# Ordering a fused attention and MLP kernel's instructions with another simulated clock

## The chip, the cores and the metric

The kernel runs on one core of a Trainium2 chip. The metric is device time in microseconds, from launch to end of one execution; the time of a kernel is the median of several runs. Five engines work side by side, each from a queue of its own: TensorE (PE, with its weight loads as PEld), VectorE (DVE), ScalarE (ACT), GpSimd (POOL) and SyncE (SP, which here only issues DMAs).

## The reference

A recurrent attention over 768 time steps for 4 batches and 8 heads of size 40, and behind it a dense MLP from 320 to 2048 to 320 over the 3072 tokens. All in float32.

```python
def _attn_ref(r, k, v, w, a, b):
    state = zeros((B, H, D, D))
    for t in range(S):
        y[:, :, t] = einsum('bhd,bhde->bhe', rt, state)
        Sa = einsum('bhde,bhe->bhd', state, at)
        state = state * wt[:, :, None, :] - einsum('bhd,bhe->bhde', Sa, bt)
        state = state + einsum('bhd,bhe->bhde', vt, kt)
    return y

def _moe_ref(x, w_in, w_out):
    h = x @ w_in
    sp = where(h > 20.0, h, log1p(exp(minimum(h, 20.0))))
    return ((h * tanh(sp)) @ w_out)
```

## The kernel before

The 768 time steps are cut into 12 chunks of 64 (`C`). Within a chunk the recurrence is solved in closed form; only the state goes from one chunk to the next. The 32 pairs of batch and head are worked on together, in halves called `be` and `al`. The names of the parts, with their lines:

- `pre_a(c, be)` (126 to 203) prepares half a chunk. SP loads `wa` and `bk` (131, 134; two buffers each). VectorE forms products of the decays by scans (147, 157) and scales the inputs (152, 170), ScalarE copies `ad` (155), POOL stores `P` to DRAM as `pD` (172), TensorE makes the 64 by 64 products `pa` (186) and transposes (202), and ScalarE and VectorE take them out (188 to 193, 203).
- `pre_inv(n)` (205 to 221) inverts triangular blocks for a pair of chunks on VectorE: a transpose (209), 30 links of two dependent instructions each (214, 216), and transposes back (218, 220). It has one buffer each for `XL`, `tmp` and `TT`. Called the solve below.
- `post_inv(n)` (223 to 260) builds the block inverses with many small matmuls (232, 241) and copies (235, 249 to 251), and makes `KT` (258, 260).
- `step(c)` (349 to 370) carries the state over chunk `c`, for two halves `g`: `step_a` (copies of the state into `VS`, 277; matmuls `pu`, 284; `UVT`, 286), `step_u` and `step_d` (transposes, 293 and 304), `step_b` (matmuls `pq`, 314; masked copy `UVQ`, 316), and `step_c` (matmuls, 334 and 339; new state `ST`, 342 and 346; output `yev`, 343). `step_loads` (265 to 271) has POOL load `VS`, `UVT` and `bdr` for the next chunk, and POOL stores `yev` to DRAM as `yD` (370).
- `Mlp` (479 to 626). Its weights come as float32 and are split into a high and a low part by `split` (489 to 495), a chain of a DMA on SP (453), ScalarE (459, 494) and VectorE (461 to 463, 495) for each of 20 pieces. `run` then goes over 6 blocks of 512 tokens: SP loads `xy` and `xp` (472 to 476), VectorE and ScalarE make `xh` and `xl` (567 to 570), and for each of 8 parts of the hidden width come 16 matmuls `ph` (584), the activation (586), the split into `gh` and `gl` (589, 590), and, three parts later, 24 matmuls `po` (604 to 606). The results are copied and stored (610, 611).

What sets the order: the program is written as one long trace in the order of `attention`'s main loop (392 to 411), where each pair of chunks runs step, preparation of the pair after next (`a`), solve of the next pair (`i`), weight work (`A`), step. The MLP stands behind all of it. The framework then makes the order of each engine's queue itself. It keeps the data's dependences and the buffers, and picks among the instructions that are ready on a simulated clock by their priority, which is the place in the trace unless a block is moved ahead. That is done by hand all over the attention:

```python
def at(tc, k):
    return tc.high_priority(offset=OFF[k]) if OFF.get(k) else nullcontext()
...
    def inv(n):
        with at(tc, 'I%d' % n), at(tc, 'I'):
            TT, T1 = pre_inv(n)
        with at(tc, 'J%d' % n):
            post_inv(n, TT, T1)
```

`OFF` (38 to 40) holds some thirty such offsets, from -150 to 600: 600 for the first solve, 300 for the others, 80 more for each; 15 to 250 for parts of a step; 600 and 400 for the two blocks of weight work. The loads and stores of the attention go to the queues named by `QS = "SGGG"`: `wa` and `bk` on SP, everything else on POOL.

Of the kernel before, what the change touches and what calls it, by code (L numbers as in the profile page):

```python
# [47 lines left out]
def layouts(inp, S=768):  # L48
    nch = S // C

    def v(x):
        return x[:, :, :S].reshape(4, 2, 2, 2, nch, C, 40)

    r, k, vv, w, a, b = (v(inp[n]) for n in 'rkvwab')
    o = {}
    wt = w.transpose(4, 2, 1, 6, 3, 0, 5).reshape(nch, 2, 2, 40, 8, C)
    wa = np.zeros(wt.shape[:4] + (1040,), np.float32)
    wa[..., :520].reshape(wt.shape[:4] + (8, 65))[..., 1:] = wt
    wa[..., 528:] = a.transpose(4, 2, 1, 6, 3, 0, 5).reshape(nch, 2, 2, 40, 512)
    o['wa'] = wa  # L60
    bt, kt = (x.transpose(4, 2, 1, 6, 3, 0, 5).reshape(nch, 2, 2, 40, 8, 1, C) for x in (b, k))
    bk = np.concatenate([bt, kt], -2)
    bk[:, 1] = np.concatenate([kt, bt], -2)[:, 1]
    o['bk'] = bk.reshape(nch, 2, 2, 40, 8, 128)
    o['rD'] = np.ascontiguousarray(r.transpose(4, 1, 6, 2, 3, 0, 5)).reshape(nch, 2, 40, 16, C)
    o['vD'] = np.ascontiguousarray(vv.transpose(4, 1, 6, 3, 0, 2, 5)).reshape(nch, 2, 40, 8, 128)
    o['vN'] = np.ascontiguousarray(vv.transpose(4, 2, 5, 3, 0, 1, 6)).reshape(nch, 2, C, 16, 40)
    p = np.arange(128)
    cst = np.zeros((128, 328), np.float32)
    cst[:, :128] = np.eye(128)  # L70
    cst[:, 128:192] = (p[:, None] % 64) < np.arange(64)
    cst[:, 192:256] = np.arange(64) < (p[:, None] // 64) * 32 + p[:, None] % 32
    cst[:, 256:296] = (p[:, None] % 64) == np.arange(40)
    cst[:, 296:328] = np.arange(32) < p[:, None] % 32
    o['cst'] = cst
    return o
# [356 lines left out]
def mlp_layouts(inp):  # L433
    wi, wo = inp['moe_w_in'], inp['moe_w_out']
    wi = wi.reshape(2, 2, 2, 40, 2048).transpose(1, 3, 0, 2, 4).reshape(320, 2048)
    a = np.empty((128, 3, 2048), wi.dtype)
    a[:, 0], a[:, 1] = wi[0:128], wi[128:256]
    a[0:64, 2] = a[64:128, 2] = wi[256:320]
    o = {'wi': a.reshape(128, 3, 4, 512).transpose(0, 2, 1, 3), 'wo': wo.reshape(16, 128, 320).transpose(1, 0, 2)}
    o = {n: np.ascontiguousarray(x).reshape(128, -1) for n, x in o.items()}  # L440

    return {n: x.view(np.int64) if x.dtype == np.float64 else x for n, x in o.items()}
# [186 lines left out]
def build(tc, I, out, nch):  # L629
    with ExitStack() as ctx:  # L630
        dp = ctx.enter_context(tc.tile_pool(name="dp", bufs=1, space=bass.MemoryType.DRAM))
        yD = dp.tile([nch, 2, 40, 2, 512], F32, name="yD")
        pD = dp.tile([nch, 2, 40, 2, 520], F32, name="pD")
        M = Mlp(ctx, tc, I, yD, pD, out)
        with ExitStack() as actx:
            attention(actx, tc, I, yD, pD, nch, M)
        M.run(nch)


def launch(**inputs):  # L640
    import concourse.bacc as bacc
    import concourse.tile as tile
    from concourse.bass_utils import run_bass_kernel_spmd

    nch = inputs['r'].shape[2] // C
    arrays = layouts(inputs, nch * C)
    arrays.update(mlp_layouts(inputs))
    nc = bacc.Bacc("TRN2", target_bir_lowering=False, num_devices=1)
    I = {n: nc.dram_tensor("in_" + n, x.shape, mybir.dt.from_np(x.dtype), kind="ExternalInput").ap() for n, x in arrays.items()}
    out = nc.dram_tensor("out_0", (nch * 256, 320), F32, kind="ExternalOutput").ap()  # L650
    with tile.TileContext(nc) as tc:
        build(tc, I, out, nch)
    res = run_bass_kernel_spmd(nc, [{"in_" + n: x for n, x in arrays.items()}], core_ids=[0]).results[0]["out_0"]
    return np.ascontiguousarray(res.reshape(nch, 4, C, 320).transpose(1, 0, 2, 3)).reshape(nch * 256, 320)
# [4 lines left out]
```

## Time and profile before

| | us |
|---|---|
| median of 3 runs | 827.55 |
| lowest and highest run | 823.36 and 829.61 |
| span of the profiled execution, first to last instruction | 821.8 |
| first matmul | 14.97 |
| first and last solve begin (line 209) | 49.9 and 368.3 |
| first and last new state (line 346) | 128.5 and 459.4 |
| first matmul of the MLP | 460.65 |

The span is the only time that is recorded of the profiled execution itself; a run's time takes in a little on both sides of it. Times in rows are microseconds from the span's start. In a timeline row stand start, length, engine, line, operation and tiles; a bracket holds the idle time of the engine before it and whose end ended it. A wait row gives the total, the number and the longest of the waits of one line for another. In the 40 slices of the page each digit is the busy share in tenths, and PEclk the TensorE clock that was granted.

The chain that ended last is TensorE for 52% of the span, ScalarE for 9%, VectorE for 7% and DMA for 3%.

### The profile page before, as it was taken

The numbers are of one execution on the slowest core, as the hardware profiler recorded it, in microseconds if no ns is written. First come the engines' busy times: TensorE is split into PE (matmuls) and PEld (weight loads), VectorE is DVE, ScalarE is ACT, GpSimd is POOL, SyncE is SP. The second block draws the span as 40 slices with busy tenths as digits, with TensorE's granted clock in tenths as the row PEclk, the third lists the DMA queues.
The fourth block names the chain that finished last, engine by engine and source line by source line (L and its number), as shares of the span: only waits on it lengthen the run. The fifth ranks groups of instructions, "written<-read, shape, count | busy, mean of one in ns | idle before, by whom it ended". The sixth has DMA issues, their size and how long they took to land.

```text
span 821.8 us, 17217 instructions
## 1 busy us (share of the span) xinstructions
PE 722.7 (88%) x7048; PEld 644.8 (78%) x7048; DVE 458.7 (56%) x957; ACT 428.7 (52%) x931; POOL 103.4 (13%) x182
## 2 busy tenths in 40 slices
PE   2635798899889889888786899999999999999997
PEld 2524697788778778788676789999999999999997
DVE  6689878749899757988954558311312212111110
ACT  5533556784586867567685555343333333432331
POOL 8100012123223022221102100000000000000000
PEclk9855679999999999999999999999999999999999
DMA  6522224323433134423528755210300100000000
GB/s 169 143 65 81 57 53 96 99 67 97 118 103 76 59 96 105 83 58 111 142 76 207 160 157 135 59 51 1 77 33 0 55 17 1 33 1 1 33 1 32
DMA packets 58206, 61.81 MB, mean 75 GB/s; under 512 B 25536, under 2 KB 48704, under 8 KB 58128
## 3 DMA queue, kind: packets, MB, share of 16 engines
q1 hardware_dynamic: 49296, 40.94, 18.3%
q0 software_dynamic: 8832, 19.79, 10.0%
q8 instruction: 55, 0.90, 0.5%
q14 instruction: 23, 0.19, 0.1%
HBM read 48.79 MB, written 11.86 MB: 74 GB/s over the span
## 4 chain that ended last, share of the span: by engine, by line
PE 52%; ACT 9%; DVE 7%; DMA 3%; issue 2%; SPq 0%; ACTq 0%; DVEq 0%
PE ph L584 21%; PE po L605 7%; PE po L604 7%; PE po L606 7%; PE pa L258 2%; PE pa L186 2%; DMA xp<-pD 1%; DVE tmp L214 1%; DVE XL L216 1%; PE pq L314 1%; ACT bdT L249 1%; PE pu L284 1%; ACT bdT L250 1%; DMA cv_d<-in_wi 1%; ACT KT L260 1%
## 5 line engine op out<-in xcount | busy, mean ns | idle before, releaser
L590 DVE TENSOR_TENSOR gl<-g,gh 128x1024 fp32r<-128x1024 f32 x48 | 58.6, 1224 | 207.5 <-ACT gh L589 207.5
L586 ACT ACTIVATE g<-ph 128x512 f32<-128x512 f32 x96 | 57.3, 598 | 180.5 <-PE ph L584 180.3
L186 PE MATMUL pa<-bk,ad 128*128 128x168 f32 x384 | 85.6, 376 | 42.8 <-DVE bk L170 15.0
L604 PE MATMUL po<-w_oh,gh 128*128 128x320 f32 x384 | 118.3, 308 | 0.0
L605 PE MATMUL po<-w_ol,gh 128*128 128x320 f32 x384 | 118.3, 308 | 0.0
L606 PE MATMUL po<-w_oh,gl 128*128 128x320 f32 x384 | 118.3, 308 | 0.0
L584 PE MATMUL ph<-xh,w_ih 128*128 128x512 f32 x288 | 112.7, 393 | 2.0 <-ACT xh L568 2.0
L186 PEld LDWEIGHTS pa<-bk,ad 128*128 128x128 f32 x384 | 71.5, 235 | 48.2 <-issue 22.8
L584 PE MATMUL ph<-xh,w_il 128*128 128x512 f32 x288 | 97.1, 391 | 0.0
L584 PE MATMUL ph<-xl,w_ih 128*128 128x512 f32 x192 | 75.1, 391 | 0.0
L605 PEld LDWEIGHTS po<-w_ol,gh 128*128 128x128 f32 x384 | 72.1, 188 | 2.2
L604 PEld LDWEIGHTS po<-w_oh,gh 128*128 128x128 f32 x384 | 72.1, 188 | 1.8
L606 PEld LDWEIGHTS po<-w_oh,gl 128*128 128x128 f32 x384 | 72.1, 188 | 0.0
L584 PEld LDWEIGHTS ph<-xh,w_ih 128*128 128x128 f32 x288 | 54.1, 188 | 12.1 <-ACT xh L568 2.2
L584 PEld LDWEIGHTS ph<-xh,w_il 128*128 128x128 f32 x288 | 54.0, 188 | 11.6 <-issue 0.2
L216 DVE TENSOR_TENSOR XL<-XL,tmp 128x30 f32<-128x30 f32 (+9 forms) x180 | 58.7, 326 | 2.4
L214 DVE TENSOR_TENSOR tmp<-XL 128x30 f32<-128x30 f32 (+9 forms) x180 | 58.2, 324 | 2.3
L258 PE MATMUL pa<-bdT,HA 128*104 128x128 f32 x384 | 52.2, 289 | 7.0 <-ACT bdT L251 5.5
L258 PEld LDWEIGHTS pa<-bdT,HA 128*104 128x104 f32 x384 | 46.7, 179 | 11.1 <-ACT bdT L251 7.2
L314 PE MATMUL pq<-bdr,UVT 128*128 128x128 f32 x384 | 53.4, 284 | 0.4 <-ACT UVT L286 0.3
L334 PE MATMUL pq<-UVQ,bkn 128*64 128x104 f32 (+1 forms) x768 | 44.7, 254 | 7.8 <-DVE UVQ L316 5.5
L589 ACT CAST gh<-g 128x1024 fp32r<-128x1024 f32 x48 | 50.1, 1048 | 1.3
(89 smaller groups left out, 1212.6 us busy)
## 6 DMA issues: line engine op xcount, KB each, us to landing
wa<-in_wa SPq DMA_DIRECT2D x48, 162.5 KB
bk<-in_bk SPq DMA_DIRECT2D x48, 160.0 KB
cv_d<-in_wi SPq DMA_DIRECT2D x12, 512.0 KB
cv_d<-in_wo SPq DMA_DIRECT2D x8, 640.0 KB
pD<-P POOLq DMA_DIRECT2D x48, 81.2 KB, 2.2
VS<-in_vN POOLq DMA_DIRECT2D x24, 160.0 KB, 3.4
UVT<-in_vD POOLq DMA_DIRECT2D x24, 160.0 KB, 3.9
bdr<-in_rD POOLq DMA_DIRECT2D x24, 160.0 KB, 4.4
```

Source lines behind the costliest of these rows:

```text
L186: PE.matmul(pt[:, j], ad[:, s0 + j].rearrange("p k a t -> p (k a t)"), bk[:, s0 + j], start=(j == 0), stop=True, skip_group_check=True)
L214: V.tensor_tensor(out=tv, in0=X[:, i + 1:32, i:i + 1].broadcast_to([128, 31 - i, i]), in1=X[:, i:i + 1, 0:i].broadcast_to([128, 31 - i, i] ...
L216: V.tensor_tensor(out=X[:, i + 1:32, 0:i], in0=X[:, i + 1:32, 0:i], in1=tv, op=ALU.add)
L258: PE.matmul(pk[:, j], ha[:, s0 + j], bd[:, s0 + j].rearrange("p a t -> p (a t)"), start=(j == 0), stop=True, skip_group_check=True)
L314: PE.matmul(pq[:, s], UVT[:, g * 4 + s, be * 128:be * 128 + 128], br[:, be, g * 4 + s].rearrange("p a t -> p (a t)"), start=(s == 0), stop ...
L584: PE.matmul(ph, w, x, start=(n == 0), stop=(n == 7), skip_group_check=True)
L586: A.activation(g[:, j], ph, AF.Mish)
L589: A.copy(gh, g)
L590: V.tensor_tensor(out=gl, in0=g, in1=gh.bitcast(F32), op=ALU.subtract)
L604: PE.matmul(po[k], gh[:, j, t], oh, start=(f == 0), stop=False, skip_group_check=True)
L605: PE.matmul(po[k], gh[:, j, t], ol, start=False, stop=False, skip_group_check=True)
L606: PE.matmul(po[k], gl[:, j, t], oh, start=False, stop=(f == 15), skip_group_check=True)
```

## The change

The framework's context gets one argument. With it, the simulated clock that drives the ordering of the instructions is that of the framework's timeline simulator instead of the simulator that it takes by default. The trace, the priorities, the tiles and their buffers stay as they are.

```diff
-    with tile.TileContext(nc) as tc:
+    with tile.TileContext(nc, schedule_with_timeline_sim=True) as tc:
         build(tc, I, out, nch)
```

## The prediction

> **What bounds the kernel now.** The page comes first, for the span, the busy shares and the 40 slices.
>
> ```profile
> span 821.8 us, 17217 instructions
> PE 722.7 (88%) x7048; PEld 644.8 (78%) x7048; DVE 458.7 (56%) x957; ACT 428.7 (52%) x931; POOL 103.4 (13%) x182
> PE   2635798899889889888786899999999999999997
> PEclk9855679999999999999999999999999999999999
> ```
>
> TensorE is busy for 722.7 us of 821.8, so 99.1 us of the span are its idle time. The slices show that these are not spread evenly: from slice 23 on it stands at 9. The stages with their busy times come next, one row for each stretch; behind the stretch come its length and then the busy time of each engine.
>
> ```profile
> core 0: us, PE busy (x) PEld busy (x) DVE busy (x) ACT busy (x) POOL busy (x), PEclk, DMA share, GB/s
> 0.00:100.00 100.00, 51.18 (x251) 43.07 (x253) 80.88 (x183) 45.23 (x123) 24.61 (x46) 0.74 0.39 106
> 40.00:100.00 60.00, 32.51 (x163) 27.23 (x165) 52.99 (x130) 24.85 (x73) 5.07 (x10) 0.63 0.24 70
> 100.00:460.00 360.00, 315.29 (x4722) 278.95 (x4716) 280.02 (x682) 246.00 (x614) 75.19 (x131) 0.97 0.38 97
> 300.00:340.00 40.00, 37.17 (x465) 33.22 (x464) 31.36 (x82) 23.76 (x66) 13.72 (x24) 1.00 0.38 92
> 340.00:380.00 40.00, 33.85 (x503) 29.89 (x502) 33.40 (x88) 27.75 (x75) 5.81 (x12) 0.96 0.34 86
> 420.00:460.00 40.00, 30.02 (x490) 26.06 (x490) 21.01 (x37) 25.22 (x52) 7.14 (x11) 1.00 0.69 158
> 460.00:480.00 20.00, 19.35 (x197) 16.02 (x198) 11.05 (x13) 10.46 (x18) 2.86 (x5) 0.91 0.66 134
> 480.00:800.00 320.00, 320.00 (x1781) 290.59 (x1780) 85.57 (x79) 123.11 (x172) 0.75 (x2) 1.00 0.14 41
> 800.00:822.00 22.00, 16.91 (x109) 16.17 (x107) 1.23 (x1) 3.95 (x7) 0.00 (x0) 0.95 0.08 30
> ```
>
> So there are three stages. The start, 0 to 100, has 48.8 us of idle TensorE (100 - 51.18), and VectorE with 80.88 is the busiest engine there. The steady part of the attention, 100 to 460, has 44.7 us of idle TensorE (360 - 315.29). The MLP from 480 on has none until the tail, which has 5.1 (22 - 16.91). Then the waits between 100 and 460 (total, times, longest), for how the idle time is made up, and the longest of TensorE's in the timeline.
>
> ```profile
> POOL pD L172 <- DVE w L150: 66.8, 6, 18.2
> POOL VS L267 <- PE pu L284: 57.7, 12, 11.8
> PE pu L293 <- ACT UVT L286: 8.1, 7, 2.6
> PE pq L334 <- DVE UVQ L316: 5.5, 4, 3.1
> ```
> ```profile
> 452.46 0.94 PE L334 MATMUL pq<-UVQ,bkn 128*64 128x104 f32 x16 [3.15 <-DVE UVQ L316]
> ```
>
> The reader is to see that TensorE's waits are many and short, at most 3.15 us: hand-overs along chains of dependent work, not an engine stuck for long behind a badly placed instruction. Long waits stand only on POOL's queue, which has room.
>
> **The change, part by part.** No instruction, byte, buffer or priority is added or removed. What can move is the place of an instruction in its engine's queue, SP's and POOL's included, since both sorts of scheduler pick among the ready instructions by the written priorities, at the instants of a simulated clock. A different clock gives different instants, so other instructions are ready when an engine comes free. The program that reaches the chip holds each engine's instructions in the order so found. The price of the change is thus a change in TensorE's idle time, stage by stage.
>
> *MLP, 480 to the end: 0 us.* TensorE is busy for all 320.00 us up to 800. All its inputs but the next x block are made by ACT (123.11 of 320) and VectorE (85.57 of 320), so those cover any order of theirs; if that cover went, a late x block would show as a TensorE gap. The tail's 5.1 us are the last copy and store, in data order. Bounds: from 0 down, since there is nothing to win, to a few tenths up.
>
> *Start, 0 to 100: 0 us, between -25.7 and +10.6.* The first steps wait for the first triangular solve (the loop of lines 211 to 216 between the transposes of lines 209 and 218). Its groups on the page, for six solves together:
>
> ```profile
> L216 DVE TENSOR_TENSOR XL<-XL,tmp 128x30 f32<-128x30 f32 (+9 forms) x180 | 58.7, 326 | 2.4
> L214 DVE TENSOR_TENSOR tmp<-XL 128x30 f32<-128x30 f32 (+9 forms) x180 | 58.2, 324 | 2.3
> L209 DVE STREAM_TRANSPOSE XL<-GP 128x1024 f32<-128x1024 f32 x6 | 12.7, 2121 | 0.0
> L218 DVE STREAM_TRANSPOSE TT<-XL 128x1024 f32<-128x1024 f32 x6 | 11.7, 1950 | 0.1
> ```
>
> One solve is (58.7 + 58.2 + 12.7 + 11.7) / 6 = 23.6 us of VectorE. In the timeline of VectorE the first one lasts from 49.93 to 99.26:
>
> ```profile
> 49.93 2.09 DVE L209 STREAM_TRANSPOSE XL<-GP 128x1024 f32<-128x1024 f32 x1
> 51.90 1.20 DVE L147 TENSOR_TENSOR_SCAN P<-wa,d 128x520 f32<-128x520 f32 x1
> 53.05 0.17 DVE L214 TENSOR_TENSOR tmp<-XL 128x30 f32<-128x30 f32 x1
> ...
> 53.14 0.16 DVE L150 COPY w<-P 128x8 f32<-128x8 f32 x1
> 53.21 0.68 DVE L152 TENSOR_TENSOR wa<-wa,P 128x512 f32<-128x512 f32 x1
> 53.81 0.20 DVE L216 TENSOR_TENSOR XL<-XL,tmp 128x30 f32<-128x30 f32 x1
> ...
> 97.33 1.93 DVE L218 STREAM_TRANSPOSE TT<-XL 128x1024 f32<-128x1024 f32 x1
> ```
>
> That is 49.3 us, 25.7 more than its own work, because work of lines 147 to 170 for later chunks stands between its links. An order without that work would win up to 25.7 us here. An order with one more stall of the longest kind costs the 10.61 us of this TensorE row:
>
> ```profile
> 60.89 4.77 PE L186 MATMUL pa<-bk,ad 128*128 128x168 f32 x16 [10.61 <-ACT ad L155]
> ```
>
> I take 0, nearest to the row of VectorE: it is busy for 52.99 of 60 us, and what is moved out of the solve has to be done soon after, by the same engine.
>
> *Steady attention, 100 to 460: +12.6 us, between -20.6 and +60.1.* TensorE has 315.29 us of work here whatever the order, so the stage lasts that long divided by its busy share. The rows bound the share. The fullest stretch, 300 to 340, has 37.17 / 40 = 0.929; at that share the stage would last 339.4 us, 20.6 less. The emptiest, 420 to 460, where VectorE too is only busy for 21.01 of 40, has 0.751: 420.1 us, 60.1 more. The present mean is 0.876. I take 340 to 380, 33.85 / 40 = 0.846, the poorest stretch in which solves, preparation and steps still run side by side: 372.6 us, 12.6 more. The reason for a value on the dear side is an asymmetry in the rows. A better order can only take from waits that are short and partly true hand-overs. A worse one puts an instruction with an unmet wait at the head of a queue and holds up everything behind it; the POOL rows show what such a wait can be, 18.2 us. Behind a `pD` store on POOL's queue stand the loads of the next step (lines 267 to 271), and the first matmuls of that step (line 284) wait for those. On SP's queue the loads of `x` stand among the weight loads in the same way; that start of the MLP lies within this stage and its bounds.
>
> *Sum.* 0 + 0 + 12.6 on the span of 821.8 gives 834.4. The median, 827.55, lies 5.75 above that span (the runs lie 1.6 to 7.8 above it), so the forecast is 827.55 + 12.6 = 840.2, taken as 840.
>
> **The rivals.** *Faster, 809 us.* Place: the last solve. Its transposes:
>
> ```profile
> 368.27 2.13 DVE L209 STREAM_TRANSPOSE XL<-GP 128x1024 f32<-128x1024 f32 x1
> ...
> 408.52 1.98 DVE L218 STREAM_TRANSPOSE TT<-XL 128x1024 f32<-128x1024 f32 x1
> ```
>
> It lasts 42.2 us, 18.6 more than its own 23.6, and the last two steps and the half-empty stretch of 420 to 460 come after it. If the new clock calls the next link ready sooner, the solve runs unmixed, the weight conversions that were mixed in go into VectorE's free 19 us of 420 to 460, and the attention ends 18.6 us sooner: 827.55 - 18.6 = 809. For it: the other work is of low urgency. Against it: the written priorities already put the solve first, and it is mixed all the same. It decides once that solve takes under 30 us.
>
> *No change, 827.6 us.* The order may come out nearly as it is, because the data fix it: twelve steps in a row, six solves in a row, single buffers. For it: 315.29 us of TensorE work and 280.02 of VectorE's in 360 leave little freedom. Against it: with several chains running beside each other, few ties have to flip. This is also the case in which the change does not do what it says.
>
> *Much slower, 888 us.* One mechanism: on POOL's queue a `pD` store of a later chunk comes ahead of the next step's loads. At 5 us for each of 12 steps that is 60, the 60.1 of the bound above: 827.55 + 60.1 = 888. For it: POOL already waits 66.8 us in six such places. Against it: today the loads land in time, and TensorE has no long wait for them. It decides when the loads are issued later than the steps ahead of them end.
>
> *The clock falls, 865 us.* TensorE was granted 0.63 where it was busy for 32.51 of 60 us, and 1.00 where it was busy for 30.02 of 40. The row of line 186 above takes 4.77 / 16 = 0.298 us for each matmul at the low clock; at the full one it is 1.98 / 12 = 0.165:
>
> ```profile
> 337.09 1.98 PE L186 MATMUL pa<-bk,ad 128*128 128x168 f32 x12
> ```
>
> If on top of the forecast the emptiest stretch fell to the low clock, its 30.02 us of work would take 30.02 x (0.298 / 0.165 - 1) = 24.2 us more: 864.4, say 865. For it: a worse order brings gaps longer than the present 3.15 us. Against it: even 0.751 busy holds 1.00. The Trainium skill, in "TensorE: Matmul & The Clock Gate", section "What's actually happening", says that the array runs at half rate after an idle window of about 3.4 us and at the full rate again after a busy one. By that rule every gap of that length would cost clock as well as the gap, which speaks against any reordering; the trace agrees so far as waits of up to 3.15 us left the clock at 1.00 and the start with its 10.61 us wait had 0.63.
>
> **How the numbers follow.** Chances: the forecast (840) 0.35, no change 0.23, faster 0.22, much slower 0.15, the clock 0.05. About 1% is what a measurement of this kernel can tell from no change, so faster (below 819) is 0.22, the same 0.23, slower (above 836) 0.35 + 0.15 + 0.05 = 0.55. The range goes from the faster rival, 808, to the much slower one, 888; about half of each of these two cases lies outside it, some 0.2 in all. The likeliest case alone reaches from 828 to 855, from no loss to about twice the forecast one.
>
> **What would show it.** Right: TensorE's busy time within 1% of 722.7, no gap from 480 us after the start of the MLP on, and 100 to 460 longer by about 13 us with more waits of 1 to 4 us. The instruction counts must be the same. A last solve of under 30 us shows the faster rival, TensorE's waits for a DMA at line 284 the much slower one, a granted clock below 0.9 between 140 and 460 the clock's. I am wrong in the stage if the difference stands in the start or the MLP, and wrong in the sign if the steady stage's busy share rises above 0.876.

## The result, and the profile after

| | before | after |
|---|---|---|
| median, us | 825.99 (4 runs, 823.36 to 829.61) | 885.17 (4 runs, 882.48 to 889.0) |
| ratio | | 1.0717, 95% interval 1.0674 to 1.0761 |
| span of the profiled execution, us | 821.8 | 880.7 |
| first and last new state (line 346), us | 128.5 and 459.4 | 152.7 and 518.7 |
| first matmul of the MLP (line 584), us | 460.65 | 519.6 |

The kernel became 7.2% slower, 59 us. The three moments in the lower rows, which are starts in the timelines, divide the 59 us: the first new state comes 24.2 us later, the way from the first to the last one takes 366.0 us instead of 330.9, 35.1 us more, and the MLP takes 361.1 us from its first matmul to the end in both kernels. The page of the kernel after, its summary lines:

```profile
span 880.7 us, 17240 instructions
PE 739.5 (84%) x7048; PEld 664.4 (75%) x7048; DVE 462.5 (53%) x957; ACT 426.1 (48%) x931; POOL 103.3 (12%) x182
PE   1675339887877989886779869999999999999997
PEclk9667659999988988998798989999999999999999
```

The counts of busy instructions on every engine are those of before. TensorE's idle time is 880.7 - 739.5 = 141.2 us instead of 99.1, 42.1 more. The other 16.8 us of the longer span are TensorE's own work: the same 7048 matmuls took 739.5 us instead of 722.7, at a mean granted clock of 0.911 instead of 0.953. The stages of the kernel after (behind the stretch come its length and the busy time of each engine), and below them the fourth stretch in the kernel before:

```profile
0.00:100.00 100.00, 54.62 (x234) 46.20 (x235) 71.76 (x159) 46.13 (x124) 25.43 (x48) 0.76 0.39 111
40.00:100.00 60.00, 38.98 (x174) 32.95 (x173) 44.64 (x108) 27.87 (x83) 6.75 (x14) 0.70 0.29 87
100.00:460.00 360.00, 280.74 (x3986) 253.00 (x3985) 266.25 (x664) 210.02 (x540) 65.89 (x116) 0.87 0.29 77
140.00:460.00 320.00, 264.02 (x3715) 237.94 (x3714) 232.85 (x582) 198.03 (x513) 64.87 (x114) 0.91 0.32 84
560.00:880.00 320.00, 315.79 (x1778) 288.12 (x1776) 79.47 (x74) 117.62 (x167) 0.00 (x0) 1.00 0.11 32
```
```profile
140.00:460.00 320.00, 278.78 (x4191) 246.23 (x4189) 247.16 (x599) 219.82 (x552) 67.48 (x117) 0.99 0.39 100
```

Compare the third busy time, VectorE's, in the first two rows: 71.76 where it was 80.88, and 44.64 where it was 52.99. The engine that paces the start stands still for 9.1 us longer in the first 100 us and so gets fewer instructions done (159 instead of 183). TensorE is not worse off in these 100 us (54.62 against 51.18); what it loses comes right behind them, when it waits for VectorE's first solve. What VectorE stands still for is in the waits of the whole kernel (total, times, longest):

```profile
POOL VS L267 <- PE pu L284: 137.7, 14, 36.2
DVE w L145 <- DMA wa<-in_wa: 40.1, 19, 4.2
DVE cv_w L461 <- ACT cv_m L459: 30.9, 16, 7.0
PE pa L232 <- DVE TT L218: 22.1, 3, 20.2
DVE bk L170 <- DMA bk<-in_bk: 16.7, 10, 3.5
PE pq L314 <- DMA bdr<-in_rD: 1.3, 2, 0.9
```

The second and the fifth row are new. In the kernel before, line 145 has no wait for `wa` that is listed at all, and line 170 has one of 0.2 us for `bk`. Together they are now 56.8 us, in 29 places. POOL waits more than before as well, but its loads for the steps come nearly in time: the last row shows that TensorE waits 1.3 us in all for `bdr`. One of the 29 places, in VectorE's timeline during the first solve:

```profile
67.24 0.30 DVE L214 TENSOR_TENSOR tmp<-XL 128x130 f32<-128x130 f32 x1
70.17 0.42 DVE L145 TENSOR_REDUCE w<-wa 128x8 f32<-128x256 f32 x1 [2.63 <-DMA wa<-in_wa]
70.50 0.28 DVE L216 TENSOR_TENSOR XL<-XL,tmp 128x130 f32<-128x130 f32 x1
```

The link of line 216 needs only the result of line 214, which is there at 67.54. It stands behind the reduce of line 145, which belongs to a later chunk and waits 2.63 us for its load. The link starts only at 70.50, behind the reduce: on this queue nothing passes an instruction that waits, so the solve waits too. Seven such waits, 13.3 us in all, fall into the first solve. It begins 5.3 us later than before, at 55.27, and lasts 65.4 us, to 120.7, where it took 49.3:

```profile
55.27 2.08 DVE L209 STREAM_TRANSPOSE XL<-GP 128x1024 f32<-128x1024 f32 x1
```
```profile
120.74 1.92 PE L232 MATMUL pa<-TT,GP 32*32 32x32 f32 x64 [20.22 <-DVE TT L218]
```

TensorE stands for 20.22 us until the solve ends; before, its longest wait of line 232 for a solve was 0.8 us. The chain of waits shows a load in front of a step too (start, length, what):

```profile
179.81 0.79 SPq L134
180.65 5.88 DMA bk<-in_bk
186.65 1.23 DVE bk L170
187.87 0.61 DVE UVQ L316
188.53 1.66 PE pq L334 x16
...
212.88 4.49 DMA wa<-in_wa
...
318.97 3.48 DMA wa<-in_wa
```

Here the load of `bk` for a later chunk is issued at 179.81 and lands 5.88 us later, the scaling of line 170 follows, and only then the copy `UVQ` of line 316, for which the present step's matmuls wait. The shares of the chain that ended last, on the page:

```profile
PE 64%; DMA 12%; ACT 8%; DVE 8%; issue 3%; SPq 1%; POOL 0%; DVEq 0%; ACTq 0%
PE ph L584 20%; PE po L606 6%; PE po L604 6%; PE po L605 6%; DMA wa<-in_wa 4%; PE pq L314 4%; PE pa L186 4%; DMA bk<-in_bk 4%; PE pa L258 3%; PE pa L202 3%; PE pq L334 3%; DMA cv_d<-in_wi 2%; PE pu L284 2%; PE pa L241 2%; PE pq L339 1%
```

Loads of `wa` and `bk` make up 4% and 4% of it, and DMA 12% instead of 3%.

Why the loads come too late can be counted in the two programs. There are two buffers of `wa`; line 170 of a half chunk is the last to read one, and line 145 of the half after next is the first to read what is loaded into it. In VectorE's queue the median number of places between the two is 17 before and 9.5 after. At a mean of 458.7 / 957 = 0.48 us for an instruction that is 8.1 us before and 4.6 us after, for a load that takes 3.4 to 5.9 us on the chain, and must be issued first.

### The profile page after: what moved, and what is told of

It reads as the page before. It is cut to its first block, busy times and chain, and to the rows that moved or that the text cites. A ratio compares the mean times of both kernels' runs of the same rounds, so it can differ in the third digit from the quotient of the medians.

```text
span 880.7 us, 17240 instructions
## 1 busy us (share of the span) xinstructions
PE 739.5 (84%) x7048; PEld 664.4 (75%) x7048; DVE 462.5 (53%) x957; ACT 426.1 (48%) x931; POOL 103.3 (12%) x182
## 3 DMA queue, kind: packets, MB, share of 16 engines
q1 hardware_dynamic: 49296, 40.94, 16.7%
## 4 chain that ended last, share of the span: by engine, by line
PE 64%; DMA 12%; ACT 8%; DVE 8%; issue 3%; SPq 1%; POOL 0%; DVEq 0%; ACTq 0%
PE ph L584 20%; PE po L606 6%; PE po L604 6%; PE po L605 6%; DMA wa<-in_wa 4%; PE pq L314 4%; PE pa L186 4%; DMA bk<-in_bk 4%; PE pa L258 3%; PE pa L202 3%; PE pq L334 3%; DMA cv_d<-in_wi 2%; PE pu L284 2%; PE pa L241 2%; PE pq L339 1%
## 5 line engine op out<-in xcount | busy, mean ns | idle before, releaser
L186 PE MATMUL pa<-bk,ad 128*128 128x168 f32 x384 | 88.5, 386 | 34.1 <-DVE bk L170 16.9
L186 PEld LDWEIGHTS pa<-bk,ad 128*128 128x128 f32 x384 | 74.7, 244 | 39.8 <-DVE HA L191 17.3
L202 PE MATMUL pa<-cst,bk 128*128 128x128 f32 x192 | 36.9, 326 | 28.9 <-DVE HA L191 21.7
L334 PE MATMUL pq<-UVQ,bkn 128*64 128x104 f32 (+1 forms) x768 | 47.0, 261 | 13.2 <-ACT yev L343 6.6
L314 PEld LDWEIGHTS pq<-bdr,UVT 128*128 128x128 f32 x384 | 51.2, 212 | 7.7 <-ACT UVT L286 5.4
## 6 DMA issues: line engine op xcount, KB each, us to landing
wa<-in_wa SPq DMA_DIRECT2D x48, 162.5 KB
```

Of the source, the lines that this page charges most:

```text
L186: PE.matmul(pt[:, j], ad[:, s0 + j].rearrange("p k a t -> p (k a t)"), bk[:, s0 + j], start=(j == 0), stop=True, skip_group_check=True)
L202: PE.transpose(pt[:, j].rearrange("p a b -> p (a b)"), bk[:, s0 + j, 0:128], ident)
L314: PE.matmul(pq[:, s], UVT[:, g * 4 + s, be * 128:be * 128 + 128], br[:, be, g * 4 + s].rearrange("p a t -> p (a t)"), start=(s == 0), stop ...
L334: PE.matmul(py[be * 64:be * 64 + 64, 2 * j + al, 0:n], BKN[c, be][:, u * 40:u * 40 + 64], UVQ[be][:, u, 0:n], start=(j == 0 and al == 0), ...
```

## The experiments

Theory A: the new clock takes a load as landed sooner than it is. So it puts the readers of `wa` and `bk` early, and VectorE stands at its queue's head with ready work behind it. Theory B: those waits lie beside slack, and the loss is in other choices that the new clock makes. Two kinds of edits tell them apart. The first writes the order out: dependences along each queue's list hold all five queues to the order of one of the two kernels, and a few instructions are moved in one list. The counts of busy instructions stay the same. An order without a move was not run, so that holding a list costs no time is not shown by a time of its own.

```diff
         build(tc, I, out, nch)
+        impose(tc, ORDERS)
...
+def impose(tc, orders):
+    ins = list(tc.nc.cur_bb.bb.instructions)
+    for o in orders:
+        for p, q in zip(o, o[1:]):
+            tc.add_manual_dep(ins[q], ins[p].name, mybir.DependencyInfo(mybir.DependencyClass.NoSync, mybir.DependencyReason.DATA), reason="order")
```

The second changes what the clock that drives the ordering thinks a DMA costs; the program on the chip gets another order and nothing else. Each ratio below is to runs of the kernel before on the same chip.

**The reduces alone (late_reduce).** The order of the kernel after, the 24 reduces moved right ahead of the reciprocal that reads them. One of the 24:

```diff
 L191 TENSOR_TENSOR HA<-pa,cst
-L145 TENSOR_REDUCE w<-wa
 L216 TENSOR_TENSOR XL<-XL,tmp
 L191 TENSOR_TENSOR HA<-pa,cst
 L214 TENSOR_TENSOR tmp<-XL
 L157 SCALAR_TENSOR_TENSOR wa<-wa,d
 L216 TENSOR_TENSOR XL<-XL,tmp
 L193 TENSOR_TENSOR GP<-GP,cst
 L191 TENSOR_TENSOR HA<-pa,cst
+L145 TENSOR_REDUCE w<-wa
 L146 RECIPROCAL d<-w
```

> All five queues stand as in the changed kernel, except that on VectorE's queue each of the 24 reductions that wait for a wa load (line 145) stands right ahead of its own reciprocal (line 146), behind the links of the solve and other work that stood between them. Theory A (the new clock takes the loads as landed sooner than they are, so VectorE stands at the head of its queue waiting for wa and bk, 56.8 us in all, with ready work behind): VectorE's wait for wa falls from 40.1 us to under 20, the time falls by 15 to 35 us, to 850 to 870. Theory B (the loss is in the other choices: TensorE's, ScalarE's and POOL's orders; VectorE's waits for loads only fill time lost anyway): the wait may fall, the time stays within 6 us of 885.

867.38 us, ratio 1.0439 (1.0395 to 1.0483). VectorE's wait for `wa` fell from 40.1 to 6.6 us, the first new state came at 142.4 instead of 152.7, and the steady part took 359.4 us instead of 366.0. So 24 small moves on one queue take 18 us of the 59 away (23 by the ratios). This is for A, but 33.5 us of waiting brought 18 to 23 us, not all of it.

**Halves of that edit (reduce_start, reduce_rest).** The same move for the first 12 reduces only, and for the last 12 only.

> The order of the changed kernel on all five queues; of its 24 reduces of line 145 only the first 12, which belong to the start, are moved right ahead of their line 146. Theory A (the loss is VectorE standing at its queue's head for loads of wa and bk while ready work is behind): what all 24 won in the start is won here alone: first new state near 142.4 us instead of 152.7, the steady part as long as in the changed kernel, so the time some 8 to 11 us below it: 873 to 878. VectorE's wait of line 145 falls from 40.1 us to 17 to 23. Theory B (the loss lies in the other choices of the order, and that wait was only lying beside it): within 4 us of 885.

> The complement: only the last 12 of the 24 reduces are moved. Theory A: first new state near 152.7 us as in the changed kernel; the steady part near 359.4 us instead of 366.0, so the time 5 to 9 us below the changed kernel: 876 to 880; this gain and that of the run on the first 12 add up to the 18 us of all 24 within 4 us. Theory B: within 4 us of 885.

879.9 us, 1.0529 (1.0442 to 1.0615), and 877.03 us, 1.052 (1.0458 to 1.0583). The first lies just above A's range, the second in it, and the first new state comes at 144.4 and 151.7 us, near what A gave. By the ratios each gains about 16 us and the whole 23, by the medians they gain 5 and 8 and the whole 18; with runs of the first from 869.17 to 882.31 us, whether they add up isn't decided. One reading is a miss: in the profiled execution of reduce_start, its quickest, the steady part took 359.2 us, as with all 24, where A gave 366.0. Moments of single executions are too coarse to tell the halves apart.

**Line 170 too (late_both, late_steady).** To late_reduce was added that line 170 goes up to six places later in VectorE's queue, past ready work; in the second run only from the 12th half chunk on.

```diff
-L170 TENSOR_TENSOR bk<-bk,wa
 L316 TENSOR_TENSOR UVQ<-pq,cst
 L316 TENSOR_TENSOR UVQ<-pq,cst
...
 L346 TENSOR_TENSOR ST<-stn,R
 L325 TENSOR_TENSOR R<-rw
+L170 TENSOR_TENSOR bk<-bk,wa
 L342 TENSOR_TENSOR stn<-ST,pq
```

> The queues of the late_reduce run, with one thing more: on VectorE's queue each of the 24 scalings that wait for a bk load (line 170) stands up to six places later, behind links of the solve, links of preparation and work of the steps that does not need it. Theory A: its wait for bk falls from 17.2 us to under 10 and the time from 867 by 4 to 15 us, to 852 to 863; what is left of the 56 us is then in instructions that the later places do not reach. Theory B: within 4 us of 867.

> All 24 reduces of line 145 moved as before, and line 170 up to 6 places later, but only from the 12th half chunk on, where it waits for the load of bk; the halves of the start keep its place, since there the move of all of them put off the first new state by 11.5 us. Theory A: first new state near 142.4 us, the steady part near 352.6 us instead of 359.4, so 5 to 9 us below the run with the reduces alone: 858 to 862. Theory B (the place of line 170 is worth nothing by itself): within 3 us of 867.

The first was a miss: 871.83 us, 1.0585 (1.053 to 1.0639). It put the first new state off from 142.4 to 153.9 us, while the steady part got shorter, from 359.4 to 352.6 us. In late_reduce line 170 waits only once for its load before the first new state, 1.29 us, so in the start the move had little to win. The second run keeps the start's places: 863.85 us, 1.038 (1.0334 to 1.0426), some 2 us above the range that A gave, 3.5 us below late_reduce by the medians and 5 by the ratios. Its queues are those of late_reduce up to the first new state, and yet that came at 146.5 us instead of 142.4, so some 4 us between moments of two profiled executions say nothing. Its waits for loads:

```profile
DVE bk L170 <- DMA bk<-in_bk: 9.3, 8, 3.0
DVE w L145 <- DMA wa<-in_wa: 5.3, 4, 2.1
```

So with 42 of the 56.8 us of waiting gone the kernel after is still 3.8% slower than before.

**The reverse (before_early_reduce).** All five queues in the order of the kernel before; 21 reduces moved on VectorE's, to the distance behind the freeing line 170 that they have in the kernel after.

```diff
 L216 TENSOR_TENSOR XL<-XL,tmp
+L145 TENSOR_REDUCE w<-wa
 L214 TENSOR_TENSOR tmp<-XL
 L216 TENSOR_TENSOR XL<-XL,tmp
...
 L191 TENSOR_TENSOR HA<-pa,cst
 L216 TENSOR_TENSOR XL<-XL,tmp
-L145 TENSOR_REDUCE w<-wa
 L214 TENSOR_TENSOR tmp<-XL
```

> All five queues in the order of the kernel before, only 21 of VectorE's reduces of line 145 moved earlier, to the distance behind the line 170 that frees their buffer which they have in the changed kernel (median 9.5 places instead of 17). Theory A: VectorE waits 20 to 45 us for loads of wa where it waited for none, and the time is 10 to 25 us longer, 837 to 852. Rival (in a good order such waits lie beside slack, and the loss of the changed kernel came with its other choices): within 5 us of before in spite of the waits.

860.61 us, 1.0391 (1.0308 to 1.0474), 32 us by the ratio (25 to 39): more than A gave. This is the cleanest of the runs, since every other place is as before. Its page and the waits of line 145:

```profile
span 859.6 us, 17218 instructions
PE 737.7 (86%) x7048; PEld 659.6 (77%) x7048; DVE 460.0 (54%) x957; ACT 428.9 (50%) x931; POOL 103.9 (12%) x182
```
```profile
DVE w L145 <- DMA wa<-in_wa: 34.4, 14, 7.8
```

34.4 us of waits, none before, and a span longer by 37.8. That is more than the 32 us of the ratio, since the profile of before shows one of its quicker executions and that of this run one of its slower ones. The reader should see that it is longer in two ways, as in the kernel after: TensorE's idle time went from 99.1 to 859.6 - 737.7 = 121.9, and its own work from 722.7 to 737.7 us, at a mean granted clock of 0.925 instead of 0.953. So stalls on VectorE show up in TensorE's time twice, as gaps and, by these two profiles, as slower matmuls.

**Dearer loads for the new clock (loads_2us, loads_2_5us, loads_3us, loads_5us).** The simulated DMAs take 2, 2.5, 3 or 5 us longer. The edit for 2:

```diff
+    import concourse.hw_specs as hs
+    hs.TRN2Spec.DGE_DMA_DELAY = {e: (650 if e in (mybir.EngineType.SP, mybir.EngineType.Pool) else 784) + 2000
+                                 for e in hs.TRN2Spec.DGE_DMA_DELAY}
     nch = inputs['r'].shape[2] // C
```

> The changed kernel, with the clock of the ordering told that every DMA lands 2 us later; nothing else differs. Theory A: with loads priced nearer to the 4 to 5 us that the trace shows, VectorE's waits for wa and bk fall from 56.8 us to under 25 and most of the 59 us come back: 825 to 850. Theory B: the other choices of the new clock remain, 870 to 900.

> The changed kernel with all DMAs priced 2.5 us later, between the two runs that gave 845 and 829.5. Theory A, if the size of the price alone decided: 830 to 842. If the particular order that comes out counts as much as the price, it may lie outside, 818 to 850.

> As before with 3 us. Theory A: VectorE's waits for wa and bk under 15 us, 805 to 840. Theory B: 870 to 900.

> The new clock with all DMAs 5 us dearer, twice what brought the loss away. Valley (a price on either side of the truth costs): 2 to 6% slower than before, 843 to 876, with load waits under 6 us. Rival (dear enough is enough, the default clock's 3.8% at twice its price was of another cause): within 1% of before.

| dearer by, us | waits for `wa` and `bk`, us | time, us | ratio, interval |
|---|---|---|---|
| 0 (after) | 40.1 and 16.7 | 885.17 | 1.0717, 1.0674 to 1.0761 |
| 2 | 6.6 and 2.4 | 844.99 | 1.0183, 1.0129 to 1.0238 |
| 2.5 | 5.4 and 1.2 | 828.7 | 1.0024, 0.9983 to 1.0066 |
| 3 | 5.8 and 3.9 | 829.55 | 1.0007, 0.9981 to 1.0033 |
| 5 | 3.4 and 0.7 | 836.91 | 1.0119, 1.005 to 1.0187 |

At 2.5 and 3 us the whole loss is gone, with the one number in the clock. 2.5 was better than expected, and 5 is worse than 3, though less than the valley theory gave and a little more than its rival did. Between 2 and 5 the waits hardly differ while the times do, so the waits for these loads are not all. With 5 us the attention is even quicker than before (last new state at 446.9 instead of 459.4), but the MLP starts at 486.8. Its page row of TensorE, and SP's queue there:

```profile
PE   1667579998889899889896179999999999999997
```
```profile
469.32 0.33 SPq L453 DMA_DIRECT2D cv_d<-in_wo  x1
471.65 0.33 SPq L472 DMA_DIRECT2D xy<-yD  x1
...
481.00 0.60 SPq L476 DMA_DIRECT2D xp<-pD  x1
```

The slice with the digit 1 is 461 to 482 us: the first `x` block is issued only behind the weight loads on SP, and TensorE has nothing. An order with this attention and the `x` loads ahead of those weights was not run.

**Which queue's loads (loads_3us_sp, loads_3us_pool).** 3 us dearer on SP's queue alone, and on POOL's alone.

```diff
+    late = {mybir.EngineType.SP: 3000, mybir.EngineType.Pool: 0}
+    hs.TRN2Spec.DGE_DMA_DELAY = {e: (650 if e in late else 784) + late.get(e, 0) for e in hs.TRN2Spec.DGE_DMA_DELAY}
```

> The changed kernel, with the clock told that DMAs of SP's queue alone (wa, bk, the weights, xy and xp) land 3 us later. Theory A: these are the loads that VectorE waits for, so most of what the 3 us on both queues gave comes back: 825 to 848. If POOL's loads of the steps (VS, UVT, bdr) were what mattered: 870 to 890.

> The same with the DMAs of POOL's queue alone. Theory A: VectorE's waits for wa and bk stay above 40 us and the time at 870 to 900. If POOL's loads were what mattered: 825 to 850.

835.24 us, 1.0129 (1.0091 to 1.0166), against 885.86 in a single run. A dearer price on POOL's queue alone brings nothing; on SP's alone it brings most of the loss back, (1.0717 - 1.0129) / 0.0717 = 82%. The rest came back only with both dearer.

**The default clock with another price (default_cheap_loads, default_dear_loads, default_1200, default_1400).** The kernel before, with the start of a simulated DMA at 0, 2600, 1200 and 1400 ns instead of 1300.

```diff
+    import concourse.hw_specs as hs
+    hs.TRN2Spec.DMA_START_FIXED_NS = 0.0
     nch = inputs['r'].shape[2] // C
```

> The kernel before, with the default clock of the ordering told that a DMA has no start-up time (1.3 us less). Theory A: the default's order shows the same illness, VectorE waits for wa and bk for 20 us or more (0.2 before) and the time rises to 845 to 880. Theory B: 818 to 838, as before.

> The kernel before with its default clock, whose fixed price of a DMA's start is doubled from 1300 to 2600 ns. Theory A says that a price too low costs and that one which is high enough costs nothing more by itself, since in the kernel before VectorE waits for loads for only 0.2 us: VectorE's waits for wa and bk stay under 4 us, and the time is within 2% of before, 812 to 845. Rival (any shift of the clock away from the one for which the offsets were chosen costs about the same, whichever way it goes): slower by 3 to 7%, 850 to 885, with waits for loads that are no longer than before.

> The kernel before with its default clock, the fixed price of a DMA's start 1200 instead of 1300 ns. Theory P (the order of before is a good one among many that this scheduler makes, because the offsets were set for it, and any other costs 0 to 4% even without load waits): 1 to 4% slower, 836 to 862, with VectorE's waits for wa and bk under 4 us. Theory A alone (only load waits cost): within 1% of before.

> The same with 1400 ns. Theory P: 1 to 4% slower, 836 to 862, load waits under 4 us. Theory A alone: within 1% of before.

| start, ns | waits for `wa` and `bk`, us | time, us | ratio, interval |
|---|---|---|---|
| 0 | 6.9 and 12.4 | 863.61 | 1.0388, 1.0347 to 1.0429 |
| 1200 | 0.2 and 0.3 | 827.09 | 1.0003, 0.9971 to 1.0035 |
| 1400 | none and 2.0 | 831.98 | 1.0058, 1.0023 to 1.0093 |
| 2600 | 0.5 and none | 863.24 | 1.0384, 1.0327 to 1.0441 |

With free loads the default clock makes waits of the same kind, 19.3 us, a third of the new clock's 56.8 and just under the 20 that A gave; the time is in A's range, but the loss, 34 us by the medians, is larger than these waits. The dear price is a miss for A: it costs as much as the cheap one with hardly a load wait. Its rival, by which any shift of the clock costs, fits this run; why a dear price costs was not traced. The miss gave a theory P, by which the order of before is a lucky one and any other costs 1 to 4%. It is a miss in its turn: other orders from a price 8% away cost 0.0 and 0.6%.

**One queue's order of before under the new clock (vector_order_of_before, tensor_order_of_before).** The list of VectorE, or of TensorE, from the kernel before is imposed as above; the clock orders the other four queues around it.

```diff
-    with tile.TileContext(nc) as tc:
+    with tile.TileContext(nc, schedule_with_timeline_sim=True) as tc:
         build(tc, I, out, nch)
+        impose(tc, ORDERS)
...
+ORDERS = [[...]]
```

> The new clock, with VectorE's queue held to the order it has in the kernel before; the other four queues are ordered by the new clock around it. If the whole loss sits in VectorE's queue: 822 to 836, load waits under 5 us. If only its load waits cost and the rest is in the other queues or in their fit to each other: 845 to 865.

> The same with TensorE's queue held to the order of before, VectorE's free. Theory A (load waits on VectorE are a cost of their own): those waits stay at 40 us or more and the time at 860 or above. If the order of TensorE's matmuls is the cause: 825 to 845 although the load waits stay.

875.75 us, 1.0585 (1.0531 to 1.064), and 921.7 us, 1.1161 (1.1128 to 1.1194). The waits for loads, of the first and of the second:

```profile
DVE w L145 <- DMA wa<-in_wa: 2.8, 2, 1.9
DVE bk L170 <- DMA bk<-in_bk: 0.8, 1, 0.8
```
```profile
DVE w L145 <- DMA wa<-in_wa: 36.6, 20, 4.1
DVE bk L170 <- DMA bk<-in_bk: 15.7, 8, 4.2
```

TensorE's order alone doesn't bring the time back: with it the load waits stay, and the kernel is slower than with either order whole. VectorE's order takes the load waits away and brings only 9 us by the medians and 11 by the ratios, which is outside both ranges that were given for it. That the other four queues, ordered by the new clock, don't fit the one list is the likely reason, but not a shown one.

**What follows.** Shown: waits for loads at the head of VectorE's queue cost about their own length where all else is in the good order (34.4 us of them, 25 to 39 us), and taking 42 of the 56.8 us out of the changed kernel gives 21 us by the medians, 28 by the ratios. Shown too: a dearer price of SP's DMAs in the clock takes most of the loss away, and of all DMAs the whole.

Open: the remaining 31 to 38 us of the changed kernel, more than half of its loss. Only 14.6 us of VectorE's load waits are left there, and neither VectorE's nor TensorE's order of before brings them back alone; the orders of ScalarE, POOL and SP were not tried alone. The traces say where this rest lies. In late_steady the first new state comes 18.0 us later than before and the steady part takes 354.3 us instead of 330.9, 23.4 more. At the start TensorE still waits 17.6 us for the end of the first solve; but it does so for 15.6 and 14.9 us in loads_2_5us and loads_3us as well, which lose nothing overall, so that wait alone is not the reason. At the end of the attention loads of the weights stand on the chain: five of `in_wi` between 395 and 445 us and one of `in_wo`, 27.9 us in all, where the kernel before has three weight loads with 12.7 us. VectorE's wait in the weight work (the third row of the waits of the kernel after, 30.9 us) was 19.0 before. No run moved those by themselves.

## Why the prediction was right or wrong

*MLP, 0 us.* Right: 361.1 us in both kernels, and the row of 560 to 880 has TensorE busy for 315.79 of 320 with the tail in it.

*Start, 0 us between -25.7 and +10.6.* Wrong, and outside its bounds: +24.2 us at the first new state, of which 5.3 are a later begin of the first solve and 16.1 its greater length. The value rested on VectorE being busy for 52.99 of 60 us, so that an order could only shift its work. But a queue in order can lose that cover: after, it is busy for 44.64. And the upper bound took one stall of TensorE as the worst case, where the engine that paces the stage is VectorE and the stalls come in a row, ten in the first 100 us.

*Steady attention, +12.6 us.* Too small, within its bounds of -20.6 and +60.1: it measured +35.1. So the sum missed 24.2 us in the start and 22.5 here, and both terms failed. The mechanism was named rightly, an instruction with an unmet wait at the head of a queue, and the dear side was rightly chosen; the size was taken from a stretch of before, 0.846 busy, which has no such wait for a load in it. From 140 to 460 the share is now 264.02 / 320 = 0.825, and was 278.78 / 320 = 0.871. The prediction also held TensorE's work constant at 315.29 us, and it grew: by 16.8 us over the kernel, at the lower clock. How much of the 35.1 us the load waits explain is open, as said above.

*The place.* The prediction looked for it on POOL's queue and, on SP's, only at the loads of `x`. It was at SP's `wa` and `bk`, seen on VectorE. A wait that is absent before has no row; that it was near could only be counted, as the 17 places of 0.48 us each for a load of 3.4 to 5.9 us.

*The rivals.* The faster one and no change didn't come. The much slower one gave 888 us, close to the 885.17, by luck, since its mechanism was hardly there: TensorE's wait for `bdr` is 1.3 us, and dearer loads on POOL's queue gave 885.86. The clock came as a companion: the granted clock is 0.91 between 140 and 460, where it was 0.99, just above the 0.9 that was named as its sign. The rule of the Trainium skill that was weighed there ("TensorE: Matmul & The Clock Gate", "What's actually happening") has half the rate follow an idle window of about 3.4 us. The trace bears it out only in the direction: in this stretch TensorE has one wait of that length (4.0 us; before none), while those of 1 to 3.4 us went from 11 to 22. TensorE's busy time didn't stay within the 1% that the prediction gave, since it is 2.3% longer.

*Chances and range.* Slower was the likeliest sign, 0.55, and 885 lies within 808 to 888, near its upper end; but that end came from POOL's queue, so that the range holds the result is luck. The likeliest case's own 828 to 855 didn't hold it.

## What to carry to other kernels

Before an order is changed, count for every double-buffered load how many instructions stand between the one that frees the buffer and the first reader, times the reader's engine's mean duration, and set that beside the load's time on the chain: where the two are near, a few places on one queue decide. The number of loads times their length is then a rough upper estimate of these waits, not of all that a new order can cost: more than half of the loss here stayed when most of the waits were gone. Where a scheduler orders by a simulated clock, the price that clock gives a load is a tuning knob of the kernel: here it was worth 7%, and a price too high cost as well as one too low. And ask of a wait what stands ready behind it: a wait of 2.63 us stood in front of a ready link of the solve that TensorE then waited for, while behind POOL's 137.7 us of waiting TensorE waited 1.3 us for `bdr`.

## What the runs showed of the hardware

A load of `wa` or `bk` took 3.40 to 5.88 us from issue to landing where it stood on the chain of the kernel after. The DMA issues of the kernel after give its size:

```profile
wa<-in_wa SPq DMA_DIRECT2D x48, 162.5 KB
```

The Trainium skill, in "DMA: Bandwidth & Descriptors", section "Anatomy of one DMA — SWDGE (gpsimd) path", has a fit of 2.0 us and the bytes at 436 GB/s; an estimate by it would be 2.4 us for these 162.5 KB. It is made for loads that GpSimd issues, while these are issued by SP; the measured times are longer, and they decide here. The same page's "Rules for kernel authors" advise to issue a load early and to wait for it late. The trace agrees with a price: 21 readers moved earlier, nothing else, cost 32 us.

Unexpected was also how little more idle time went with a lower granted clock: in the kernel with the early reduces 22.8 us more of idle TensorE came with a mean clock of 0.925 instead of 0.953, and with 15.0 us more for the same 7048 matmuls. The clock of one kernel is spread, too: the four executions with the early reduces had 0.925 to 0.937, and all but one of the 52 executions of the kernel before that were run beside the experiments had 0.933 to 0.956. So a part of the 15.0 us can be this spread.
